# A new order table for a one-core attention and two-layer MLP kernel, drawn with other TensorE durations for the float32 tiles

## The chip, the cores and the metric

The kernel runs on one core of a Trainium2 chip. The metric is the device time of one execution in microseconds (us), given as the median over several runs; lower is better. The profile is of one execution on that core. Its engines are TensorE (PE), VectorE (DVE), ScalarE (ACT), GpSimd (POOL) and SyncE (SP), which only issues DMAs here.

## The reference

```python
q_bucket, k_bucket = sign bits of (q @ proj), (k @ proj), 6 bits each
mask = q_bucket[:, :, :, None] == k_bucket[:, :, None, :]
scores = np.where(mask, q @ k.T / sqrt(64), -1e9)
attn = softmax(scores)
x = (attn @ v)                       # 2 batches, 8 heads, 768 tokens, head size 64
x = x.transpose(0, 2, 1, 3).reshape(1536, 512)
h = maximum(maximum(x @ w1, x @ w2), x @ w3) @ w_out        # 512 -> 768 -> 512
out = elu(h @ w_in) @ w_out2                                 # 512 -> 2048 -> 512
```

Everything is float32 at the interface. The kernel computes products of float32 operands as three float16 products of split halves (high times high, high times low, low times high).

## The kernel before

**Work.** Attention runs over 24 units (`u`: six chunks `c` of 256 tokens, three to a batch, with four pairs of heads `p` each), and each unit has four tiles of 128 queries, so 96 tiles. `plan_tile` (L598 on) writes one tile: four matmuls of scores into one of two score buffers in PSUM (`scores`, L617), the row maximum on DVE (L623), two tiny DVE steps for scale and bias (L624, L626), the exponential on ACT (L628), a float16 high half (L657 on ACT or L659 on DVE), a subtraction for the low half (L663 on POOL or DVE), a DMA transpose issued by SP (L665, tile `PT`), and 18 matmuls with V (L671 to L673). The four tiles of a unit share one output buffer `o` (one buffer in the ring); L689 to L693 scale it, L695 and L696 split it, and an SP transpose (L699) makes the chunk's `xT`.

**The float32 path.** Units 0 to 3 (`u < FU`, FU = 4: tiles 0 to 15) take another way after the exponential: six PE transposes of the float32 tile back into the score buffer (`turn32`, L638/L640), a copy to SBUF (L644), and twelve float32 matmuls with V as loaded (`pv32`, L647/L649).

**V.** `plan_v` loads one pair of heads (L491). In batch 1 all four pairs go through one buffer, `rawv`. A pair's load waits for the split of the pair before (L499, L501); then follow a squared sum on ACT (L332), a one-column matmul that adds it over partitions (`sumsq`, L279/L280), a power-of-two scale (L317, L319) and the split. The first unit of a batch cannot be scaled (L689) before all four pairs of that batch have their scale (L510 to L515).

**The rest.** Each of the six chunks goes through `plan_moe1`: 18 groups of up projections and four of down projections, all by line 712 (12 matmuls of 256 columns for an up group, 18 for a down group), evacuated by L733 to L769; below, U2.0 is the first up-projection group of chunk 2, D1.2 the third down-projection group of chunk 1. Weights are made into float16 halves by L534 to L559. After attention, `plan_moe2` runs 96 groups of 12 matmuls (L712), an ELU chain (L831 to L840) and six matmuls of 512 columns each (L847).

**What sets the order.** Planning gives a list of 3359 operations. `Graph.emit` decompresses `ORDER` into 3359 words; each is an operation's number times eight plus the engine that runs it. Operations are emitted in that order, each to its engine's queue. All queues are in order, and ring buffers are handed out in table order, so the table fixes what stands behind what on each engine. The costs written beside the operations (`PE32T`, `PE32V`, `act`, `gtt` and the others) go into the operation list but `emit` does not read them.

```python
for t, w in enumerate(todo):
    o, e = self.ops[w >> 3], ENGINES[w & 7]
    ...
    o["fn"](e)
```

Of the kernel before, what the change touches and what calls it, by code (L numbers as in the profile page):

```python
# [101 lines left out]

ENGINES = ("PE", "V", "A", "G", "D", "N")
ORDER = (
    "c-l2rOITXx))u_6@y5m*;Ejz}&?w*yh#EknY&6Qo8=DvfOj5BOh&=<b8Hmk5YzE@VKx_w+(}CCy#C9N_4ub7KOb22+5Zi&+48)Uxm=46|f1ZDBdd|!Dt;@UKwKljfU`35Yro!pZ76>PE#r@9H<@K@s"
# [3 lines left out]
    "-85~BIM9u;%Pqe<?lJGapAM`Blejk_+Ud;~$h08vVa7wx^q$!+Q5F~DCG8@0JD;(*0c^$nvp~qNMT2sS=<0`=P;l0MdM-{9{m1TbuC627C|6Zc^GxtBiHLzpj_^MfTsiSj9mX_g1Su7L`#9Rz7C(NC"
    "$IR1<+i{6*_Ol`6`H6~Fv%DG%k#62AmN|TGiJ0%AU28@wE}j<7&PqHsuaC3QMnp01d(NIxKL2@i+b{ZRA2WSWScSIhz|x`Q#^s)QV_#UD^Qf+txi7+)QsYR9I2FIfqw}uCt)2Z3eX7m)8Vy<L^?8=D"  # L110
    "e-i8vGnwrVygE4u4e|VkU;RW**_Kw6X1ZJB#mmEW+b`{Y!uZoM{Wr(f#wN*)L}Qi@vE}b9(>Fdt=!kZRp!!d(r{e91e|7R1@5>9_Eh7*-j@=+M1Qkl&l1?^$I(<S+3%*V+w#_4c)XX@%s6D^f$oxZo"
    "rJyG<nyj;X^Y1=a;V5@AuEInN7s^}ncz=Aofcmb2D<We^9G3HivOTlpoV8(Ce<5>}FRetqYNyNnUix8Qt~XnEAMS8*&nxUrm%(;EzsSXeQm=3$(D!T5D~b9PswDru>HDMT`!A+e4y`Y37n?p!_=IM6"
    "EXLxy*URgE6-}n}{-QqG!3mNR!Tyi=n*IB(udnNIQPdI(oKzh8T)|Kz2|>BK8{PD$jAv)3+x`HXrd<mnB!{f|Qu4Kq<eR4iqPO&8+q~S|H?6vvwn>Dy`zv<ZCV!S0d?l3Fkq_R5Q*_48`{SMLf>1fM"
    "W6ob#8UfecCO-ENwO6Fsi%iS@6K|qp!X1_>`A^2eEXuv&(m&HI!$;b9e!}+3&M#bB7Yf~;>iWky@-}8kn$1}A{k-6h`)E$4%j15ziLr|jbl+<bN^X{eJAJr$W$=~gm*-ZSsc3#|d(HYWY1_0fZhMw|"
    "ep%p9=|2wm7q2+WZ;rnB{RAFU5iA}HtCMshi6nCTQqG7HzeRV+3U-@Fr!)uNifIU2_s#WR+_j%ljLsk_!>3%kYU7#BzVMZ1d8H3?dujsiV2JlMVX<mSllkRJ`Ic|$->2u^mAUDp1-Hlhcx|w5=Rfe*"
    "6#Qe&=Je3^j$i*c#b6$IX1zZ2WNY@bJ>4@dCORX{*1ho0$0v~}Tz2rF+?f0GI({MkS>$jwKF8b62HCUUxvp;ZL(v=Bo7cZ`q<1ml<{=-Rj=9lT{3Nm-P|iCDdY9~oSz}t#MU~cY<k)6^A(8W>-YB}b"
    "j9>jLuE{N?8IaC@nyrT`GSxQw+xeINuVkuE`3pFYaGsPO8?S_caInth-jvAAH*aak_VLHpe{K8&<%R!<EAgfEly`f_Vl_buG#0qfFXnn{hc-TSxlNv?tsREL>GkcobZ1vq8VaB3*}qA%+iLr1ZPpWb"
    "<C!1hc;|c$*;!N?yCh!R-3#y!77cNFfT`K&GF#s)<l5%NUSB92xnB0~|N5r*A{H0P4*#MtRUt91(H)(h|Gs^~UvYdPSK)fnABfIfD1|}KF`c|IOBP<n-m_1OR%pm4@;}y49_~ycDlFt#JdV6W1s3k?"
    "TGCAIl0;C`glOXMZ1pe+czoqe6Xd7QM4MYXjcw+WX^(mZ&e+b?zkfR0vz|n@qp^)%*^dkUpBd48ug~_G|M}JNE#0thKDf!q3x%yV7HxhpqU2&OvGBu%RQ?98C>6f+rT*)qFATAl<~WTsSveSU6ZHut"
    "Q-}V*Wax0^ldE`9^!@KNq5>h{1hLn`Z`WiCDi2P)=3$@9uT<V;=XW)(lRe|vfje|oXZd)p?<P9qcm?nGAAH)y)^{~L*OxztnRBm$@W+xx|J3CwB?dhIwCSaJdVXQsW{bwo<0^bjv9wCGZS21DdZq$&"  # L120
    "<CclBJ`;QqB2TTT4|m#a#2G_Pa?hhNwQTP-d^N4kvx44Gc;Pk@i(gu3JO?Jd76_+oN;<OSBD7kj@L=r&i+!|1nhEYSW_dVc|Jvu@aA>!@r#sHG-GC?<I1Jd~n_hb1j@)<_jj^acCijxGZ)^NPi*<G="
    "36UHf?T5wA)AOh<grE^c>^3Si#srqNR~)}<%SN;M{5~5)>9-<umq3Kt%?7S!CqUn~OFp-n<Uzr)agMM$BtI;ns_%Pe9nQs-r5cILw*JaHubcIqL|6-NiY#$CPhfX4-SANO>}*x8#@+JH@SbJbhI;Za"
    "@Ad^ja(7+pQA~u}W1b&R4nu)`+I}z?J~;pBlBp587ndA+vo84CU-DvcnkjVc+4zFDg19{Kqf^@StbN+yM8xucdL^g1s;!+6OTdlQ9ItuSq?=)dKM>?=4^^CV_*oL#*$V{m0C9R|SDoAj6(NyS{+ly;"
    "q0&Zn13|su`gZY*j3HBm;Wk1`4o4AmcAn-4iDu@VtKuv7qSG~NX>wmEOwPFamM$$4A}B8Kz;{h-V_UAqBz$6Z&&x9^@p9{aaBgu~cIgXo39?454TUA~KL~OX<?a%$dAIrEMkx1KXZ8<6o8h%@lt%O7"
    "vWL!0LS0<xlva<CwPLf)Y`vl*@lSt#eIC7XGud1$d@Qm%&JT~n(Ku~8qG(+3#xO)Zx4as$MgvQV=zHJl`oXdL2KB%_Bl7tDF^xw5+N&bGK89@9XlC222zeT@*?E2}c%+S93+ohWRh%X~J;zzkUDvvW"
    "sM#2cC-DSAi&V0*ZpGK{N~|=U5+%*H4TIhF%ImW@ygv2x-kwCh*69l{Ub*G^z*b-xZkA;ZX|pd1M4AJW&wuj;JTYmAed+gUr+qzsvN7wh_d3om1HtK7d`lPHv7ONomVe9Ta9##H+y3*_OV@S0jjwfk"
    "kAlC5q#k+r`g|o$tD%Q5=>@TN?NQ;1O%)R*ZVfc28$nN|5U#gqM};%?W&_S(=r@jeetXY~qTDmb%)V1k21AOdD{weZz&H3G3fGtXD>c3oAwr86_=eLJ+r6bD>!caw{fo`j?+Q&uUtm8bIaG(jH*z|;"
    "X)t4ROq3fpSp`DtWsMikrAw_{cqz8IX%Y97G8~29rgo;)vkY$4?P0z8#^$@yI=I{ZE&X?-WopTcS!d$5)%7ip_w`{gDMb5p4$dKC2V3`BMaN-acN_f?`(^Ba&BFo_p@bVfKDB9rES^5>i$n!6q3o}t"
# [24 lines left out]


# [818 lines left out]
```

## Time and profile before

| | |
|---|---|
| median of 3 runs | 678.61 us (676.53 to 683.07) |
| the profiled execution | 676.07 us |
| its span, first to last instruction | 673.8 us |
| mean granted TensorE clock | 0.981 of full speed |
| PE, DVE, ACT, POOL busy | 633.0, 547.0, 443.0, 205.0 us |

Busy is the time in which an engine had an instruction in work. A wait is put down to the engine that released it. PEclk is the granted share of TensorE's full clock of 2.4 GHz; 0.50 is its other level, 1.2 GHz. Tile names are the program's, without buffer numbers.

### The profile page before, as it was taken

To read this page: it belongs to the slowest core of one execution; us is meant where nothing else is said; L and a number is where in the kernel's file an instruction comes from. 1 tells how busy PE (TensorE), PEld (TensorE's weight loads), DVE (VectorE), ACT (ScalarE), POOL (GpSimd) and SP (SyncE) were. 2 spreads that over 40 slices of the span, in tenths; PEclk is the share of its full clock that TensorE was granted. 3 is DMA by queue.
4 is the path that set the end of the run, shared out by engine and by line. 5 is a ranking of instruction groups with operands and counts; after the bars stand their busy time and mean duration, and the time that the engine had idled before them with its cause. 6 is when DMAs were issued, how large, how long until landed. Compare 5 with 4: busy or idle time off the path is not lost.

```text
span 673.8 us, 16505 instructions
## 1 busy us (share of the span) xinstructions
PE 633.0 (94%) x6414; PEld 493.8 (73%) x6414; DVE 547.0 (81%) x1538; ACT 443.0 (66%) x825; POOL 205.0 (30%) x184
## 2 busy tenths in 40 slices
...
GB/s 257 270 162 143 130 231 222 176 139 186 134 138 159 153 41 158 167 192 164 156 145 145 225 142 123 96 70 88 64 1 64 94 2 1 1 1 1 33 79 78
DMA packets 176030, 81.35 MB, mean 121 GB/s; under 512 B 142672, under 2 KB 170320, under 8 KB 175952
## 3 DMA queue, kind: packets, MB, share of 16 engines
...
q8 instruction: 50, 0.82, 0.5%
...
## 4 chain that ended last, share of the span: by engine, by line
PE 62%; DVE 3%; DMA 2%; ACT 2%; issue 1%; POOL 0%; DVEq 0%; ACTq 0%; POOLq 0%; SPq 0%
PE mo L712 36%; PE out L847 18%; PE s L620 4%; DMA PT<-hl 1%; PE o L671 1%; PE o L672 1%; PE o L673 1%; DVE m L623 1%; ACT junk L332 1%; DMA rawv<-in_v_dram 0%; ACT P L628 0%; ACT hl L657 0%; DVE dc L545 0%; PE mo L409 0%; DVE hl L663 0%
## 5 line engine op out<-in xcount | busy, mean ns | idle before, releaser
L712 PE MATMUL mo<-xT,w 128*128 128x256 f16 x1296 | 154.9, 275 | 2.8 <-DVE vs L317 2.4
L712 PEld LDWEIGHTS <-w 128*128 128x128 f16 x1296 | 125.3, 99 | 21.5 <-issue 3.8
L663 POOL TENSOR_TENSOR hl<-P,hl 128x768 f16<-128x768 f32 x66 | 109.2, 1663 | 99.6 <-ACT hl L657 58.4
L712 PE MATMUL mo<-x1T,win 128*128 128x256 f16 x1152 | 136.2, 273 | 0.0
L847 PE MATMUL out<-wo2t,gt 128*128 128x512 f16 x576 | 134.7, 379 | 0.0
L712 PEld LDWEIGHTS <-win 128*128 128x128 f16 x1152 | 111.8, 98 | 23.7
L628 ACT ACTIVATE P<-s,bias,scale 128x768 f32<-128x768 f32 x96 | 94.7, 988 | 37.5 <-DVE bias L626 22.3
L840 POOL TENSOR_TENSOR gt<-g,gt 128x256 f16<-128x256 f32 x49 | 34.9, 718 | 231.5 <-DVE gt L838 111.7
L623 DVE TENSOR_REDUCE m<-s 128x1 f32<-128x768 f32 x96 | 91.0, 950 | 12.2 <-PE s L620 11.7
L847 PEld LDWEIGHTS <-gt 128*128 128x128 f16 x576 | 55.2, 98 | 53.6
L831 ACT ACTIVATE r<-mo,nih 128x256 f32<-128x256 f32 x96 | 44.5, 468 | 70.4 <-PE mo L712 66.3
L657 ACT CAST hl<-P 128x768 f16<-128x768 f32 x65 | 53.1, 829 | 16.9 <-DMA PT<-hl 15.0
L834 DVE TENSOR_SCALAR uu<-e,sg 128x256 f32<-128x256 f32 x96 | 36.9, 387 | 26.7 <-ACT e L833 26.4
L671 PE MATMUL o<-vt,PT 128*128 128x65 f16 x480 | 52.8, 196 | 4.4 <-DMA PT<-hl 2.3
L620 PE MATMUL s<-ka,qa 128*128 128x384 f16 x192 | 48.7, 336 | 5.3 <-ACT P L628 3.5
L672 PE MATMUL o<-vt,PT 128*128 128x64 f16 x480 | 52.8, 197 | 0.0
L673 PE MATMUL o<-vt,PT 128*128 128x65 f16 x480 | 52.6, 195 | 0.0
L671 PEld LDWEIGHTS <-PT 128*128 128x128 f16 x480 | 45.5, 99 | 5.9 <-DMA PT<-hl 3.3
L620 PE MATMUL s<-kb,qb 76*128 76x384 f16 x192 | 49.1, 338 | 0.5 <-DMA qb<-btq 0.5
L836 DVE SCALAR_TENSOR_TENSOR g<-mo,aj,uu 128x256 f32<-128x256 f32 x96 | 45.8, 480 | 4.4 <-POOL gt L840 0.5
L672 PEld LDWEIGHTS <-PT 128*128 128x128 f16 x480 | 45.4, 99 | 3.9 <-issue 2.2
L673 PEld LDWEIGHTS <-PT 128*128 128x128 f16 x480 | 45.5, 101 | 0.0
...
## 6 DMA issues: line engine op xcount, KB each, us to landing
...
```

What stands on the lines that cost most here:

```text
L620: PE.matmul(ps.ap[:, h, :NK], lh[0:n, h0 + i, j], rh[0:n, i, h * CH:(h + 1) * CH], start=first, stop=not first)
L623: op({"V": vred(S)}, lambda e: V.tensor_reduce(out=m.ap, in_=ps.ap[:, :, :NK], op=ALU.max, axis=AX.XY), rd=[ps], wr=[m], prio=t + 80.5)
L628: op({"A": act(S, ap=2, acc=int(u < FU)) - 42}, lambda e: A.activation(out=P.ap.rearrange("p (c n) -> p c n", c=2), in_=ps.ap[:, :, :NK], ...
L657: A.copy(hl.ap[:, 0], P.ap)
L663: op({"G": gtt(S), "V": (vtt(S), -109.46)}, lambda e: eng[e].tensor_tensor(out=hl.ap[:, 1], in0=P.ap, in1=hl.ap[:, 0], op=ALU.subtract), r ...
L671: PE.matmul(oo, pt.ap[:, kt], vt.ap[:, i, kt, :D + 1], start=(kt == 0), stop=False)
L672: PE.matmul(oo[:, :D], pt.ap[:, kt], vt.ap[:, i, kt, D + 2:], start=False, stop=False)
L673: PE.matmul(oo, pt.ap[:, NS + kt], vt.ap[:, i, kt, :D + 1], start=False, stop=(kt == NS - 1))
L712: PE.matmul(o, lh(kk, x), rh(kk, y), start=(kk == 0 and pi == 0), stop=(kk == n - 1 and pi == 2))
L831: op({"A": act(NQ, ap=1) - 42}, lambda e, m=m, o=o, r=r: A.activation(out=r.ap, in_=o.ap[:, :NQ], func=AF.Relu, scale=nih.ap[:, m:m + 1]), ...
L836: op({"V": vstt(NQ)}, lambda e, m=m, o=o, uu=uu, gg=gg: V.scalar_tensor_tensor(out=gg.ap, in0=o.ap[:, :NQ], scalar=aj.ap[:, m:m + 1], in1= ...
L847: PE.matmul(outs[j].ap, gt.ap[:, x, j * 128:(j + 1) * 128], wo2t[f].ap[:, y], start=(len(seen) == 1 and pi == 0), stop=(len(seen) == n and ...
```

## The change

The string `ORDER` is replaced as a whole, and one line of constants changes. Nothing else does: the 3359 operations, the buffers and the ring sizes are the same.

```diff
 ENGINES = ("PE", "V", "A", "G", "D", "N")
 ORDER = (
-    "c-l2rOITXx))u_6@y5m*;Ejz}&?w*yh#EknY&6Qo8=DvfOj5BOh&=<b8Hmk5YzE@VKx_w+(}CCy#C9N_4ub7KOb22+5Zi&+48)Uxm=46|f1ZDBdd|!Dt;@UKwKljfU`35Yro!pZ76>PE#r@9H<@K@s"
...
+    "c-lQyOITXx))u_6@y5m*8*gm9vC$at$|h<6O~OWvfLG8cV48~QKx_wMG7y`A*bKyzf!Gejb|AI`@pK@z1F;>5?LbTiVmlB|2I9#;Ob3#a|9Sqk&H4Yezi)l-`>uDb4UgNcWz6SqKV$!(5=mvVN=j#N"
...
 )
...
 TINY = 70
 FU = 4
-PE32T, PE32V = 250, 140
+PE32T, PE32V = 140, 222
 KAPPA = 5.35559
```

Decompressed word by word, the two tables differ as follows. PE runs the same 694 operations in another order.

| operations on | before | after |
|---|---|---|
| DVE | 1533 | 1488 |
| ACT (with its DMA issues) | 753 (30) | 776 (20) |
| POOL | 169 | 181 |
| SP | 208 | 218 |

Moves by kind: the high half of a tile (L657/L659) ACT to DVE 14, DVE to ACT 11; the low half (L663) POOL to DVE 8, DVE to POOL 11; the halves of the ELU (L838) ACT to DVE 20, DVE to ACT 29, and (L840) POOL to DVE 22, DVE to POOL 30; the subtraction of a down projection (L769) POOL to DVE 2, DVE to POOL 5; weight words (L538/L539) ACT to DVE 8, DVE to ACT 20.

Places in the table, 0 to 3358, that the prediction speaks of:

| | before | after |
|---|---|---|
| second V pair of batch 1: load, squared sum, its matmul | 952, 1010, 1037 | 996, 1032, 1094 |
| last V pair of batch 1 to be loaded (p = 2): split before it, load, squared sum, its matmul | 1339, 1340, 1341, 1342 | 1205, 1212, 1243, 1281 |
| first PV matmuls behind it that need `o` (tile 52) | 1351 | 1313 |
| the two subtractions L769 of chunk 0's first down-projection groups, engine | 1030 and 1033, DVE | 974 and 1066, POOL |
| U1.4 | 1043 | 988 |
| first up group of chunk 0 and the PE operation ahead of it that is no small group | 552, tile 22's scores | 539, tile 20's scores |

Between the last load (1212) and its matmul (1281) PE's queue now has D1.2, D1.3, three PV, two scores, U2.0, U2.1, U2.2 and four small groups; between that matmul and tile 52's PV it has two scores, one PV, a small group, U2.3 and U2.4.

## Rows read from the trace of the kernel before

**Rows 1.** The page's first part: busy time, share and instructions of each engine.
```profile
PE 633.0 (94%) x6414; PEld 493.8 (73%) x6414; DVE 547.0 (81%) x1538; ACT 443.0 (66%) x825; POOL 205.0 (30%) x184
```

**Rows 2.** Busy time by stretch; the first line names the columns.
```profile
core 0: us, PE busy (x) PEld busy (x) DVE busy (x) ACT busy (x) POOL busy (x), PEclk, DMA share, GB/s
50.00:88.00 38.00, 33.42 (x304) 28.54 (x302) 36.61 (x97) 35.40 (x62) 8.06 (x7) 1.00 0.53 161
101.00:140.00 39.00, 37.28 (x500) 31.34 (x498) 37.05 (x95) 35.36 (x56) 22.61 (x15) 1.00 0.90 192
157.10:226.90 69.80, 62.75 (x855) 52.61 (x852) 55.87 (x147) 50.63 (x81) 33.24 (x23) 0.95 0.70 149
181.20:188.00 6.80, 4.22 (x20) 2.64 (x21) 5.62 (x13) 2.65 (x3) 6.08 (x4) 0.50 0.54 127
190.00:240.00 50.00, 49.37 (x614) 42.15 (x612) 39.70 (x99) 37.62 (x60) 22.74 (x17) 1.00 0.66 138
246.10:256.30 10.20, 5.48 (x79) 4.72 (x79) 3.62 (x14) 1.87 (x3) 0.00 (x0) 0.50 0.45 86
262.00:378.00 116.00, 114.57 (x1530) 97.88 (x1528) 91.72 (x227) 72.88 (x111) 64.84 (x46) 1.00 0.82 170
378.00:520.00 142.00, 141.88 (x1137) 106.39 (x1136) 121.67 (x379) 99.96 (x226) 20.86 (x26) 1.00 0.28 88
```

**Rows 3.** PE's waits from 174 to 190 us: total us, times, longest.
```profile
PE mo L444 <- DVE bitsk L440: 2.9, 1, 2.9
PE mo L712 <- DVE vs L317: 2.4, 1, 2.4
PE o L671 <- DMA PT<-hl: 1.1, 1, 1.1
```

**Rows 4.** Timeline, 181 to 184 us: start, us, engine, line.
```profile
181.10 0.72 DVE L769 TENSOR_TENSOR x1T<-hx,x1T 128x512 f16<-128x512 f32 x1
181.19 2.12 POOL L663 TENSOR_TENSOR hl<-P,hl 128x768 f16<-128x768 f32 x1 [10.17 <-ACT hl L657]
...
181.86 2.00 DVE L769 TENSOR_TENSOR x1T<-hx,x1T 128x512 f16<-128x512 f32 x1
...
183.91 0.14 DVE L317 TENSOR_SCALAR vs<-mo 128x1 int32<-128x1 int32 x1
```

**Rows 5.** PE's waits from 240 to 262 us.
```profile
PE mo L279 <- ACT junk L332: 5.4, 1, 5.4
PE o L671 <- DVE xf L693: 2.0, 1, 2.0
```

**Rows 6.** Timeline, 243 to 252 us.
```profile
243.69 1.01 DVE L501 SCALAR_TENSOR_TENSOR vt<-rawv,vs,vt 128x768 f16<-128x768 f32 x1
244.72 0.41 SPq L491 DMA_DIRECT2D rawv<-in_v_dram  x1
247.88 0.84 ACT L332 ACTIVATE junk<-rawv 128x768 bf16<-128x768 f32 x1 [4.52 <-DMA rawv<-in_v_dram]
...
248.87 0.16 PE L279 MATMUL mo<-vacc,ones 128*128 128x1 bf16 x1 [5.35 <-ACT junk L332]
...
251.02 0.21 PE L671 MATMUL o<-vt,PT 128*128 128x65 f16 x1 [1.95 <-DVE xf L693]
```

**Rows 7.** The chain that ended last: start, us, what.
```profile
205.51 1.31 PE mo L712 x12
...
214.35 1.97 PE mo L712 x18
...
252.22 4.74 DMA PT<-hl
```

**Rows 8.** Groups by line: busy us, mean ns, then idle before.
```profile
L649 PE MATMUL o<-wot,hl 128*128 128x64 f32 x192 | 23.4, 273 | 0.0
L640 PE MATMUL s<-ident,P 128*128 128x128 f32 x96 | 13.9, 286 | 0.6 <-ACT P L628 0.4
L838 DVE CAST gt<-g 128x256 f16<-128x256 f32 x59 | 16.8, 288 | 2.5 <-DVE g L836 0.5
L838 ACT CAST gt<-g 128x256 f16<-128x256 f32 x37 | 14.6, 400 | 25.4 <-DVE g L836 21.0 <-DVE o2s L319 1.6 <-PE out L847 1.6
```

More of the change, by code (lines that the diff above doesn't have):

```diff
@@ L109 @@
[L109 to L128, printed above, removed]
@@ new lines @@
+    "UYZxbaC_pfyb0VH#K#-Q{hL!L@yD)|EQI>ufz@F1o3Y)KSzPaUb6yn;&OCQ6#%A5uPUiA=F1Li6?m6)kt}A@s`|GDDxx3zQy0__k`*)Pktj44}ISg~}>3gp*<Qw!iGxo@|sC-`@Q!JXP_>nHIxOP*_"
+    "Roys4;5BgO2-XzyrGa()oa>XK<R4~Lxc8|EI}ljad@;UnBlI%6^yj&H^Wo2!Qu8#Vo)4?^$Ajj`nQkc>NxwSwYa@oM^Xr)5<jv$~%S=CJet`#PhOHjtEoUn5s|h=ro!;|W@x8w$dEq%b?pO%!FK+mj"
+    "jf9(3>+yuV&Mn`%EOrszj_*Z&R52#^FqUg;o{R3!U?F@3f8jFCi@%xwT^e?~E`Ih{CB%yjw?`r;HWya+13O+)9Xi;FD%7^{*}KR~Dzc`~z0$Q`gmw)Rp)0fPa^eU3kMZ}D_9eH>G2==2O1Y#N_D(NQ"
+    "{-3qR1fAm-<E+zVUNIRQJF5tSPPn6-#a_?GyKM}!e7MHlfvrioIT+fb7@H?ZU;;hWJ?C4mt+orZpp1;$ncFtw<+JpFSRDMFm<%bcClb6`T6JbmVE&tOIQ7WV(BJ3^3sVZe4L;_e;zK$1Lmh4ttHao-"
@@ new lines @@
+    "?r68UmJ`Jd5!Ibqk(n2qpcb^!_PJO{WD|xB&z72xH_uRW#4X{!u*Rp5W&E4f8O9g07oIP#7ffC+xv8jq=kr^acNEcp?ZA$IKzVx}bx8c%OI$vGqMMu}V&*?wYf|r}L+&<DM?P$L3|k4#^*LqdKUC`Y"
+    "{DrS$g0ZmfUqt+i+(2&}^Bu$z74DgD#;K##F{AER+s2=p>|=v#-C~b8u$?yx*XB~+p`P)I`60@6ZT@PlKKlANwu2oEBH@2du+YeN=Letr&-wlUH;DYAeSWkWGf3WFGxwJni70YLoJ;WqvPvm8Cs;jG"
+    "u9Nyp<;=gltn?Wl6^ifdeu*02vV!7uJ}P)A(XeJqi3u4z0^vneY%W~2oeerJS9F}c=>N=zH>AIj2xYE4vu<PW7XQGVE{q5WKln*m?V!@Fx3x#tf+}KW)lk>zF?oNSQ^n-I!*lP1ukA;FLhM4ecN}+r"
+    "rRr2O77w)J2KFoD^|fuAnH1JU%zr7OcE|1l#nmNr8e*1$;32YfJ@qwOhHbDI<Hu7z;j`!3H}8?nIrO{8DHpzNU?Q*`3|c-HXvLQXGr^YDJr}LTIkM#=Wq^0}x;d!F(2!bcJrPXcx~i>X$(eyvp4jRa"
@@ new lines @@
+    "?c#sQm~Ot=bB<3Kl(UKJ-m~x3Z^hAtS*iB#tr*vK&M-Vnm}Y#4O}*L~CMPdDf8oSmFzhn61Djp=fd5X^uDTX2PM7?Lr*5xlL352TeLd@b>t5TijdieWN71ykxlK>!>%lGmJa)ueuf@6B$G9R;y&Q=6"
+    "ep4*`b?6Tkm=glgnCHM-7Sd|0val^;bg^cLZ^CtRzRk<%?>jNc-uGOk{67?5_f=e$q*XD-5t+^SD)gu2h4x5fus>CE-<;}H)V8s7))ZJ-Fld6WywheZv}S&c=t?KX7mgE7BGu98GIBM(_(eQ68<E<k"
+    "#N?TBaR#L@caLz@BQ`9$PnW$O-bVEAt@G%Vv#xnLcI?@Zc)ZVizMh>IyK!cGkM$dlV*A=@gW2jhy>#L`zZ^xUeiE}yJFaWH)pl)XeEEmsvi8p0@5JswobeLj3jTSF%tzLJ{=hZk5Yc7-u@a7Oc?cd|"
+    "Kt)nQd$8&MN4vT(%9km><(Do}N4jqU$HD4aGW_Q9eUi~ElPRwRM+)lc7lgEp95l}(d@DM$st}&fO5jEQx#b6^+O4muce&&1(;lr!wHc>QHX;ni*0R&!GP{1VT5VGk$GvZ*9xwIl=d4rT4vM{+`4Sh`"
@@ new lines @@
+    "`tMw>Jdf_3GIhq6yl8CI8)vf5V*+9?7?&N*4l?%5R-H}44uvDx@acbBnNeT0&lO67e@r{bRj*R^m5+N!>7y^zMrDC_Oe+Y#I{Vh}u58o4=U@C!;C%5jG<Xz?9}@=(DMjiG39qOAVozUN!VJWGysSp~"
+    "I)hn+|7&((-c{xHJUyMrS#*267avY1?QiSXCsZ3YhqEIA*;?N6Y##g3!Jo{RJD1OAF=6D_XlxMPrYz4d?^g-w??-$4X4`kyOpev-^V=AqnP<D<Nc4OU3)VK{bBZ)sOcGbVsG2_@O@~VAD~5jElf!<+"
+    "^Sw4M>Tqh@A2=YS=+w;EXV|+hk1pd3guC$P@?Ww^_(QmS%r7k?J*TtI9g+Qw%k6dS8!gpqPd6^VupXT{m!{8s(VyMdN(Lg3IHvi#zF<fz6DbDa{+)l<QnO}j?q6rot9bV3%;kFJ=KRvC+^gBvjT-~6"
+    "PFTSi(@W2!6@7i$+#dDDSu4IB>aE*@$!xe@H4|ePh$XLXH#p;X6AHg)a`?5Di&^};sw;&-6B&;)=3V>C!&`?o`xUa~XKTzB4tI4!Hx!=GPtIX>#Cz)C1rGMMaUu{r$G6<#NHi8>bYB0UcLol_Qjgzj"
@@ new lines @@
+    "BSik7GXX(sNuvcjJUNSKjS@6!iOF4lYd{+H*?7yA_txb^59<RvwzlE(Zv}-0R57UDvrh%Z6H+ps#KeR;htp(ToDkZMR_4}}#txB`ocH?XkEdMP9ouvyI%9EgX8FRwE2m|`{>w2T-G@iY<|OSoj<X$)"
+    "*XMqQF8zAp)WuKdT&|T(43D|vd*=s7S8OFUFLvSNwx8NFd}e}&<3ve#!=B*8lx_9s#O^r#F`#xc5W7QiaYfF|@tqr6ucc@HFBStXkH8gYh-(jm9Cr30&R-{AD|bR6O1HJ+6xBuo!R7N4<-v(uNu3TJ"
+    "g?U%ebG_j`1Bo4TBiQ)Vlr^>;2!;c}(`fwtjKfJ>z7H{$m<Xyw+?ERo;zThVpPb<f<}j!0>(#_EDXL=_<SO`m9NUzecJ`z)6@hu;nxM`rTKP5<{@3=naPQ!{nrWbPQh371b4$oN6DGFU<n$aesfhd="
+    "#Z(Kf_1~95?zIGpi7Fy$_V=6buMnM1XyjHIaEBSg?Yjp~$q}Kk=^bI$vggELF;Cc5#FvrT1u41YR;uP-Uc6iKcv)O>T3vU>$7MwH$ZYlL_l?^to?5B*+U)fQ?gS6ra_iKyqm!ub>cqQfJ^N`l5?zVK"
```

53 lines of the change are left out of this document (27 added, 26 removed).

## The prediction

> **What bounds the kernel now.** I read the page's totals first: PE is busy 633.0 of 673.8 us [rows 1], so a new order of the same operations can at most take away PE's idle time and what PE lost at its lower clock. Second, busy time by stretch shows where that is [rows 2]. From 378 us on (378 to 520: 141.88 of 142 us) PE has no gap, so 296 us of the span can only get worse; 262 to 378 (114.57 of 116) and 190 to 240 (49.37 of 50) are nearly as full. Before 140 us PE is not the limit: from 50 to 88 us DVE is busy 36.61 of 38 us and ACT 35.40, PE 33.42; from 101 to 140 DVE 37.05 of 39. What is left are two holes, 174 to 190 and 240 to 262. Third, PE's waits there, and fourth the timeline, to see what each wait hangs on.
>
> First hole: waits of 2.9 + 2.4 + 1.1 = 6.4 us [rows 3]. The 2.4 us ends when DVE gets to L317, 0.14 us of work that frees the PSUM buffer for U1.4; DVE is late because two subtractions of L769 stand ahead of it, the second of which took 2.00 us where the first took 0.72, while POOL ran L663 (2.12 us) [rows 4]. In this hole the clock fell to its 1.2 GHz level: from 181.2 to 188.0 us PEclk is 0.50, and PE was busy 4.22 us of that [rows 2], so 2.1 us were lost by the clock. Sum: 8.5 us.
>
> Second hole: waits of 5.4 + 2.0 = 7.4 us [rows 5]. The timeline is plain: the split L501 ends at 244.70, the load of the next V pair is issued at 244.72, its squared sum starts at 247.88, its matmul at 248.87, and the PV matmul that needs `o` at 251.02 [rows 6]. These operations stand directly behind one another in the old table (places 1339 to 1342, 1351), so nothing on PE covers the load. Here PEclk is 0.50 from 246.1 to 256.3 with 5.48 us busy [rows 2]: 2.7 us lost. Sum: 10.1 us.
>
> **The change part by part.** No operation is added or removed; what counts is what stands ahead of what.
>
> The second hole. The new table splits the last-but-one pair at 1205, issues the load at 1212, squares at 1243 and adds at 1281. The price to hide is 4.15 us, from the issue at 244.72 to the matmul at 248.87 [rows 6]. Between load and matmul PE's queue has two down groups of 1.97 us and three up groups of 1.31 [rows 7]: 7.9 us, and three PV and two scores beside. That covers it with over 3 us to spare even if the load landed as late as the slow transposes do (4.74 us [rows 7] instead of some 3.1). From the matmul to the next `o`, 2.15 us are needed (248.87 to 251.02), and PE has two up groups, 2.6 us, with two scores and a PV. If this cover fails for want of DVE (it is the same queue L501 stands in), all 10.1 us return. I take -10.1 us; ends -10.1 and 0. SP now issues this load at 1212; behind it SP holds the chunk's `xT` transpose (1228). SP waits there for the split at 1205, which is 7 places older: I cost it at nothing, covered by the 7.9 us; if the split is late, the transpose is late by the same and U2.0 with it.
>
> The first hole. Both L769 go to POOL, earlier and later (974, 1066), U1.4 moves ahead (988), and the V pair's load, squared sum and matmul lie at 996, 1032, 1094 with many PE groups between. Between the matmuls of the key bits and their transpose (the 2.9 us wait) there are now an up group and a PV, some 1.9 us, where there was a PV. So the 2.4 and the 2.1 of the clock go, of the 2.9 I leave 1.0, and the 1.1 (a transpose that lands late) I leave too. Sum -8.5 + 2.1 = -6.4; ends -8.5 and 0.
>
> The float32 stage and chunk 0. The new costs do not reach the chip but shape the table: the trace has 23.4 / 16 = 1.46 us busy for the twelve matmuls of a `pv32` and 13.9 / 16 = 0.87 for the six transposes [rows 8], against 0.84 and 1.50 us in the old constants, 1.33 and 0.84 in the new. But the stage is DVE's and ACT's [rows 2], and what the table puts ahead there counts. Adding for every operation its own duration less its overlap (for one that moves, the mean of its kind on the other engine), DVE has 81.5 us of work ahead of tile 20's scores in the old table and 81.6 in the new, ACT 77.7 and 79.1: nothing gained. Ahead of the last up group of chunk 0, at 140 us, DVE has 127.3 and now 124.5, ACT 122.7 and 120.5. So some 2.5 us less work of the two bound engines, with the same PE work done. Against it: PE, in order, now reaches chunk 0's first up group directly behind tile 20's scores, and waits for its `xT`. Behind it stand tile 22's and 23's scores, for which DVE and ACT wait. The chain to it from the last `pv32` is three short steps (L693, L695, L696) and a transpose, with some 3.5 us of PE work beside it (two scores, a `gram` and small groups, at 0.65 us for a tile's scores); the short steps take about half of that, so with a transpose of 4.74 us [rows 7] it would be some 3 us late, part of it under DVE work that is due anyway. I take -2 us; ends -5 and +3.
>
> From 262 us. The halves of the ELU are spread anew, net 9 of L838 to ACT (0.400 us instead of 0.288 [rows 8]) and 8 of L840 to POOL. All DVE work falls by some 19 us, ACT's rises by 15, POOL's by 12. While PE is full and ACT busy 99.96 of 142 us [rows 2], this is hidden; it costs if a chain into the next product gets longer than the groups beside it, at most one group of 1.31 us each time. I take +0.5 us; ends 0 and +4.
>
> Waits that the new order makes elsewhere: before, 190 to 240 us had 0.63 us of PE idle and 262 to 378 had 1.43 [rows 2], so a drawing costs about that much where it goes well. I saw no pair of operations in the new table as tight as load, square and matmul were. +1 us; ends 0 and +9 (one hole like the first).
>
> Sum: -10.1 - 6.4 - 2 + 0.5 + 1 = -17.0 us, on the profiled execution's 676.07: 659.1. That execution lies 2.54 us under the median of the runs shown, 678.61; taken off the median, the forecast is 661.6 us.
>
> **A rule weighed.** POOL gets twelve more subtractions. In the row, a two-input subtraction on DVE took 2.00 us beside POOL's, not 0.72, so 1.28 more [rows 4]. The Trainium skill ("SBUF — State Buffer", section "Who interferes with whom") says that a DVE instruction with two SBUF inputs and a GpSimd one that reads SBUF exclude each other, the later one standing still to the end. That row agrees with it, in that DVE's ended 0.55 us after POOL's. By that rule the sum would be the third rival's.
>
> **The rivals.**
> (1) A new hole. Queues shift, and one chain, most likely scores to transposed tile in the stretch 157 to 227 us, opens a wait like the first hole with its fall of the clock: +8.5. For it: a tile there passes five engines and two DMA queues in order, and one late operation holds all behind it; in both holes the clock fell after waits of a few us. Against: the chains have more PE work between them than before. Time: 661.6 + 8.5 = 670.1.
> (2) All given back, by the engines that bound the float32 stage: ACT and DVE lose there what I count as gained (+3 for -2, so +5), chunk 0's first up groups stall once more with a fall of the clock (+8.5), and the late chains cost 4 for 0.5: 661.6 + 17 = 678.6, no change. For it: ACT gets 15 us more work, and it was at 35.40 of 38 us. Against: only some 1.4 us of that stand ahead of tile 20.
> (3) Slower, by POOL and DVE shutting each other out. Place: between tile 40's scores and U2.0, where POOL's work rises from 30.2 to 38.4 us by the table and DVE's falls from 58.8 to 46.2. If none of it overlapped, the stretch would need 38.4 + 46.2 = 84.6 us; by the forecast it takes 69.8 - 8.5 + 2.1 = 63.4. That is +21.2, and the second hole's gain is then lost as well, since its chain runs over DVE: 661.6 + 21.2 + 10.1 = 692.9. It ends slower than before once 17 of these 31.3 us are paid. Against: in the old stretch DVE 55.87 + POOL 33.24 = 89.1 us fit into 69.8 [rows 2], so at least 19.3 us did overlap. As some overlap will stay, I put the rival at 688.
>
> **How the numbers follow.** The forecast's own ends: all at their best, 661.6 - 2.1 - 3 - 0.5 - 1 = 655.0, less some 5 us for the spread of single runs (676.53 to 683.07 before), 650; at the other side 667, with a few of the small terms at their worse end. Its chance is 0.63. Rival 1, 667 to 672: 0.17. Rival 2, 672 to 685: 0.13. Rival 3: 0.07. A measurement of this kernel tells about 1%, 6.8 us, from no change. Faster by more than that (under 671.8): 0.63 + 0.17 = 0.80. Same: 0.13. Slower: 0.07. The range leaves out rival 3, the upper half of rival 2 and a little at the bottom, 0.18 in all: 649 to 676. The cases of the other sign hold little, so the likeliest one's own range is 650 to 667 within it.
>
> **What would show it.** Right: no wait of PE on L332 behind a `rawv` load over 1 us; no wait on L317 or L440 over 2 us between 160 and 190 us; PEclk 1.00 in both stretches; the span from the first ELU group to the end unchanged, about 270 us, so that the gain stands before 378 us; DVE still over 0.93 busy from 50 to 130 us. Wrong: a PEclk of 0.50 somewhere after 100 us, a wait of PE over 2 us there, or idle PE time after 378 us. A time under 650 would mean that the float32 stage got shorter, which I hold to be bound by DVE.

## The result, and the profile after

The new table takes 646.15 us (median of 4 runs, 644.94 to 649.86) against 677.78 for the kernel before beside it (4 runs, 676.53 to 683.07): a ratio of 0.9528, 95% interval 0.9464 to 0.9593. Faster, as forecast, but by nearly twice as much as forecast (661.6), and below the range (649 to 676). The profiled execution took 646.06 us, its span is 644.3; before, 676.07 and 673.8. So 30.0 us have to be found. (After, and in some of the runs, line numbers are higher by one, since the string takes a line more: L333 there is L332 before.)

The page's totals and its row of PE slices, after; they answer to [rows 1]:

```profile
PE 624.7 (97%) x6414; PEld 490.8 (76%) x6414; DVE 528.0 (82%) x1493; ACT 454.8 (71%) x858; POOL 218.5 (34%) x196
...
PE   4999889999999999999999999999999999999997
```

PE's busy time fell by 8.3 us though it runs the same 6414 matmuls. Some 6.3 of that is work no longer done at 1.2 GHz: before, PE was busy 15.9 us in its three stretches at half clock, which cost half of that; after, 3.3 us in one. The other 2.0 are not traced. The rest of the gain, 21.7 us, is idle time. DVE lost 19 us of work, ACT gained 12 and POOL 13.5, much as the counts of the tables said.

Busy time by stretch shows where. To compare like with like I cut both runs at the same PE operations: the last up group of chunk 0 (140.3 us before, 131.9 after), the first of chunk 1 (160.1 and 152.9), U2.0 (226.9 and 209.2), tile 70's scores (282.2 and 250.2), the first ELU group (403.9 and 374.1). The work between two cuts is nearly the same, not quite, as the orders differ (748 and 795 matmuls in one row). After:

```profile
core 0: us, PE busy (x) PEld busy (x) DVE busy (x) ACT busy (x) POOL busy (x), PEclk, DMA share, GB/s
50.00:88.00 38.00, 33.56 (x301) 28.57 (x300) 36.58 (x102) 37.16 (x65) 9.38 (x9) 0.98 0.67 183
88.00:132.00 44.00, 43.76 (x563) 37.09 (x563) 42.84 (x115) 43.69 (x70) 29.75 (x20) 0.97 1.00 202
152.90:209.20 56.30, 55.78 (x748) 47.70 (x746) 47.34 (x121) 47.91 (x79) 36.40 (x27) 1.00 0.96 181
209.20:250.20 41.00, 41.00 (x553) 34.96 (x552) 36.34 (x95) 29.96 (x47) 24.97 (x18) 1.00 0.77 153
250.20:374.10 123.90, 123.83 (x1539) 107.75 (x1536) 97.11 (x249) 83.09 (x141) 53.60 (x37) 1.00 0.72 166
```

The same cuts in the kernel before:

```profile
88.00:140.30 52.30, 47.77 (x584) 38.59 (x583) 49.93 (x131) 48.30 (x75) 29.77 (x20) 0.93 0.91 195
160.10:226.90 66.80, 59.75 (x795) 50.14 (x791) 53.22 (x138) 48.18 (x77) 30.24 (x22) 0.95 0.72 154
226.90:282.20 55.30, 46.85 (x570) 39.43 (x567) 37.44 (x94) 31.27 (x46) 26.52 (x19) 0.91 0.65 128
282.20:403.90 121.70, 120.67 (x1502) 104.31 (x1499) 96.24 (x250) 79.35 (x131) 52.19 (x38) 1.00 0.72 166
```

Read each row as span less PE busy. Both holes are gone: idle 0.52 and 0.00 us after, 7.05 and 8.45 before. And a third place that I had not counted as a hole has gone with them: from 88 us to the end of chunk 0 PE is busy 43.76 of 44 us, where it was busy 47.77 of 52.3, part of that at half clock. From 50 to 88 us nothing changed in kind (33.42 of 38 before [rows 2]).

PE's waits over the whole run, after: total, times, longest.

```profile
PE mo L297 <- DMA rawq<-in_q_dram: 3.7, 1, 3.7
PE s L621 <- ACT P L629: 1.9, 2, 1.6
PE s L641 <- ACT P L629: 1.7, 4, 0.8
```

The first is the start of the kernel. Nothing here answers to [rows 3] or [rows 5]; between 152 and 190 us PE waits for nothing at all. The V chain of the second hole [rows 6] now reads, in the timeline after:

```profile
201.68 0.54 SPq L492 DMA_DIRECT2D rawv<-in_v_dram  x1
206.56 0.84 ACT L333 ACTIVATE junk<-rawv 128x768 bf16<-128x768 f32 x1
213.09 0.17 PE L280 MATMUL mo<-vacc,ones 128*128 128x1 bf16 x1
```

From issue to matmul 11.41 us pass where 4.15 passed before, and none of it shows on PE: the matmul has no idle time before it. What was late before is early now by being started earlier.

**One measure for all runs.** To place a gain or a loss in a table with another order, I use the time that PE has lost by the start of a given group: its start less the full-clock durations (means from the trace of before) of all PE work that the table places ahead of it. Other durations shift a whole column alike, so what counts is how two rows differ. Worked out so for the profiled execution of each kernel, in us:

| | tile 20 | last up group, chunk 0 | first, chunk 1 | U2.0 | tile 70 | output group 90 |
|---|---|---|---|---|---|---|
| before | 31.6 | 38.2 | 39.2 | 49.2 | 61.1 | 63.1 |
| after | 29.3 | 30.4 | 31.0 | 32.1 | 32.4 | 33.5 |
| new engines, old places | 48.6 | 67.6 | 74.4 | 87.5 | 104.2 | 132.3 |
| new places, old engines | 42.5 | 51.8 | 58.2 | 66.3 | 72.2 | 102.1 |
| new to 924, then old | 32.1 | 33.8 | 34.4 | 46.9 | 58.3 | 61.7 |
| old to 909, then new | 34.4 | 46.7 | 48.5 | 49.4 | 49.8 | 51.8 |
| old, V chain early | 31.7 | 38.3 | 39.4 | 50.0 | 56.1 | 57.8 |
| old, L769 on POOL | 32.0 | 38.5 | 39.4 | 48.7 | 60.7 | 62.4 |
| new to 536, then old | 32.1 | 44.6 | 46.1 | 56.9 | 68.9 | 70.5 |
| old to 549, then new | 31.9 | 37.7 | 38.3 | 38.9 | 39.2 | 40.9 |
| new, four up groups late | 28.2 | 34.3 | 34.9 | 35.3 | 35.7 | 37.3 |
| new, V chain late | 27.5 | 30.4 | 30.9 | 32.4 | 39.2 | 40.7 |
| old, both mends | 31.3 | 37.8 | 39.0 | 48.2 | 54.0 | 55.5 |
| new, old ELU engines | 27.3 | 29.3 | 29.8 | 30.9 | 31.3 | 39.4 |

The first two lines give the gain by stretch: 2.3 to tile 20, 5.5 from there to the end of chunk 0, 0.4 to chunk 1, 8.9 in the stretch of the first hole, 11.6 in that of the second, 0.9 behind: 29.6 of the 30.0 us.

### The profile page after: what moved, and what is told of

It is laid out like the page before. It is cut to its first block, busy times and chain, and to the rows that moved or that the text cites. A ratio compares the mean times of both kernels' runs of the same rounds, so it can differ in the third digit from the quotient of the medians.

```text
span 644.3 us, 16489 instructions
## 1 busy us (share of the span) xinstructions
PE 624.7 (97%) x6414; PEld 490.8 (76%) x6414; DVE 528.0 (82%) x1493; ACT 454.8 (71%) x858; POOL 218.5 (34%) x196
## 4 chain that ended last, share of the span: by engine, by line
PE 80%; DVE 4%; ACT 4%; DMA 3%; issue 1%; POOL 0%; DVEq 0%; SPq 0%; ACTq 0%
PE mo L713 47%; PE out L848 19%; PE s L621 6%; PE o L672 2%; PE o L673 2%; PE o L674 2%; ACT P L629 1%; DVE m L624 1%; DMA kb<-ka 1%; DMA rawv<-in_v_dram 1%; PE mo L410 1%; DMA PT<-hl 1%; ACT hl L645 1%; DVE hx L734 0%; ACT mo L535 0%
## 5 line engine op out<-in xcount | busy, mean ns | idle before, releaser
L713 PE MATMUL mo<-xT,w 128*128 128x256 f16 x1296 | 152.6, 272 | 0.0
L664 POOL TENSOR_TENSOR hl<-P,hl 128x768 f16<-128x768 f32 x69 | 115.0, 1674 | 64.9 <-ACT hl L658 31.5
L713 PEld LDWEIGHTS <-w 128*128 128x128 f16 x1296 | 123.6, 98 | 16.7
L841 POOL TENSOR_TENSOR gt<-g,gt 128x256 f16<-128x256 f32 x57 | 39.3, 695 | 213.2 <-ACT gt L839 125.4
L624 DVE TENSOR_REDUCE m<-s 128x1 f32<-128x768 f32 x96 | 91.1, 951 | 12.6 <-PE s L621 11.2
L835 DVE TENSOR_SCALAR uu<-e,sg 128x256 f32<-128x256 f32 x96 | 35.5, 371 | 26.3 <-ACT e L834 25.7
L658 ACT CAST hl<-P 128x768 f16<-128x768 f32 x62 | 50.7, 830 | 2.9 <-DMA PT<-hl 2.4
L672 PE MATMUL o<-vt,PT 128*128 128x65 f16 x480 | 51.3, 193 | 0.2
L673 PE MATMUL o<-vt,PT 128*128 128x64 f16 x480 | 51.3, 194 | 0.0
L674 PE MATMUL o<-vt,PT 128*128 128x65 f16 x480 | 51.1, 192 | 0.0
L837 DVE SCALAR_TENSOR_TENSOR g<-mo,aj,uu 128x256 f32<-128x256 f32 x96 | 46.1, 482 | 6.0 <-POOL gt L841 2.0
L621 PE MATMUL s<-kb,qb 76*128 76x384 f16 x192 | 48.2, 332 | 1.0 <-DMA kb<-ka 1.0
L672 PEld LDWEIGHTS <-PT 128*128 128x128 f16 x480 | 44.4, 96 | 2.7 <-DMA PT<-hl 0.4
L673 PEld LDWEIGHTS <-PT 128*128 128x128 f16 x480 | 44.3, 97 | 2.1
L713 PEld LDWEIGHTS <-wot 128*128 128x128 f16 x432 | 41.4, 98 | 5.6
```

Of the source, the lines that this page charges most:

```text
L621: PE.matmul(ps.ap[:, h, :NK], lh[0:n, h0 + i, j], rh[0:n, i, h * CH:(h + 1) * CH], start=first, stop=not first)
L624: op({"V": vred(S)}, lambda e: V.tensor_reduce(out=m.ap, in_=ps.ap[:, :, :NK], op=ALU.max, axis=AX.XY), rd=[ps], wr=[m], prio=t + 80.5)
L658: A.copy(hl.ap[:, 0], P.ap)
L664: op({"G": gtt(S), "V": (vtt(S), -109.46)}, lambda e: eng[e].tensor_tensor(out=hl.ap[:, 1], in0=P.ap, in1=hl.ap[:, 0], op=ALU.subtract), r ...
L672: PE.matmul(oo, pt.ap[:, kt], vt.ap[:, i, kt, :D + 1], start=(kt == 0), stop=False)
L673: PE.matmul(oo[:, :D], pt.ap[:, kt], vt.ap[:, i, kt, D + 2:], start=False, stop=False)
```

## The experiments

Two theories stood at first. The places alone: what stands ahead of what makes the gain, and the engines that changed hands are incidental. The engines alone: DVE was relieved, and the order is incidental. Each was given half of the change.

**New engines, old places.**

```diff
 every entry at its place in the old table
-V L838 ... (and 360 other operations, each on its old engine)
+A L838 ... (on its engine in the new table)
```

> The old table's places with the new table's engines: each operation stands where it stood before, but runs on the engine the new table names. Theory A (places make the gain): the second hole stays whole, since load, squared sum and matmul of the last V pair still stand side by side (10 us lost there); the first loses the wait behind the two L769, which now run on POOL, at most 4.5 us with the clock; the stage before 140 us gains at most 2. About 672 us, ratio 0.985 to 1.00. Theory B (the 19 us less DVE work make the gain): the float32 stage, bound by DVE, gets shorter and the waits on DVE go: 655 us or less, ratio 0.97 or less.

Measured: 737.41 us, ratio 1.0842 (1.0772 to 1.0912). **New places, old engines**, the mirror image:

```diff
 every operation on its engine in the old table
-its place in the old table
+its place in the new table
```

> The new table's places with the old table's engines. Theory A: nearly the whole gain stays, 646 to 654 us, ratio 0.955 to 0.965; PE's wait on L333/L332 behind a rawv load is under 1 us and no stretch after 100 us is at 1.2 GHz. Theory B: most of the gain goes, 665 us or more, ratio 0.98 or more, with DVE busy 547 us as before.

Measured: 712.3 us, ratio 1.0442 (1.0386 to 1.0498). PE's waits in the first:

```profile
PE s L620 <- ACT P L628: 22.5, 21, 3.5
PE mo L279 <- ACT junk L332: 7.4, 4, 5.5
```

and in the second:

```profile
PE s L621 <- ACT P L629: 11.1, 12, 2.1
...
PE out L848 <- DVE gt L841: 3.2, 3, 2.3
```

Either half of the change alone makes the kernel slower by 8 and by 4%. Tile after tile the scores wait for the exponential of an earlier one. Both theories fall, the one of the engines by the first run and the one of the places by the second: a place is drawn for the engine that an operation has, since on an engine in order it stands behind that engine's other work, and one half of a table is no table.

**Cutting the table in two.** The first 924 entries new, then the old order and engines for what is left:

```diff
-c[0:924] of the old table
+c[0:924] of the new table
 all entries not among these, in the old order
```

> The first 924 entries of the new table (up to tile 40's scores, with all of chunk 0's up and down groups), then everything else in the old table's order. If the stages add up, as the two traces have it: the time to the first up group of chunk 1 falls by some 8 us (160.1 to 152 us) and both holes come back, 668 to 671 us, ratio 0.985 to 0.99. If the head only shifts work that is paid later, the time is 676 or more; if it is the cause of the rest, under 660.

Measured: 673.11 us, ratio 0.9877 (0.9839 to 0.9914). And the first 909 old, the rest new:

```diff
 c[0:909] of the old table
-all entries not among these, in the old order
+all entries not among these, in the new order
```

> The first 909 entries of the old table, then everything else in the new table's order: the counterpart of the run before. If the stages add up: both holes gone (some 21 us), the head as before (tile 40's scores at about 157 us), 654 to 658 us, ratio 0.965 to 0.97. If the head is what keeps the holes shut: 665 or more, with a wait of PE over 2 us after 160 us.

Measured: 659.51 us, ratio 0.9687 (0.9633 to 0.9741). In the first both holes are back, by PE's waits:

```profile
PE mo L280 <- ACT junk L333: 5.2, 1, 5.2
...
PE mo L445 <- DVE bitsk L441: 3.6, 1, 3.6
PE mo L713 <- DVE vs L318: 2.4, 1, 2.4
```

In the second, from 160 to 262 us, this is all:

```profile
PE s L620 <- ACT P L628: 0.5, 1, 0.5
PE mo L430 <- DVE hx L765: 0.5, 1, 0.5
```

So the stretches earn for themselves, if each has both halves of its own table: 8.4 us in the head and 21.3 behind it by the ratios (of 680.21, the kernel before beside these runs), together 29.7, near the 32.0 that the change gives by its own.

**The second hole, from both sides.** In the old table I moved only the chain early, with the six small DVE operations behind it that end in the scaling of `o`:

```diff
-1339 V L501   1340 D L491   1341 A L330   1342 PE L276   1343 V L317 ...
+1247 V L501   1247 D L491   1277 A L330   1307 PE L276   1307 V L317 ...
```

> The old table with one chain moved: the split of the last-but-one V pair (L499, L501), the load of the next (L491), its squared sum (L330), its matmul (L276) and its release (L317, L319), which stood at 1339 to 1344, go to 1247 to 1308, and the six DVE operations of the unit behind them to 1308; nothing else moves and no engine changes. If the second hole was this chain standing side by side, the wait of 5.4 us on L332 and the half clock of 246.1 to 256.3 us go and the time falls by 8 to 10 us, to about 669. If the hole only shows that the whole stretch is late on DVE or ACT, the wait moves to the next scores or PV and the time falls by less than 3 us.

Measured: 673.03 us, ratio 0.9884 (0.9819 to 0.9949), 7.9 us by the ratio. PE's waits from 235 to 265 us:

```profile
PE s L620 <- ACT P L628: 2.6, 2, 1.4
PE o L671 <- DMA PT<-hl: 1.3, 1, 1.3
```

The 5.4 us wait is gone, and so is the half clock of 246.1 to 256.3 us. But smaller waits come up behind it: from U2.0 to tile 70 PE now loses 6.1 us, where it lost 11.9. The mirror image in the new table, the chain and what stands behind it put side by side again:

```diff
-1205 V L501   1212 D L491   1243 A L330   1281 PE L276   1284 V L317 ...
+1304 V L501   1304 D L491   1304 A L330   1304 PE L276   1304 V L317 ...
```

> The new table with the last V pair's chain side by side again: the split L501 (1205), the load (1212), squared sum (1243), matmul (1281) and its release, and the six DVE operations behind it, all at 1304, ahead of tile 52's PV at 1313. If the distance in the table is what closed the second hole, the wait on L332 is back with some 4 to 5.4 us, the clock falls, and 7 to 10 us are lost (about 655). If the new order closes it because PE's queue stands further behind the other engines, the load lands under PE's backlog and under 3 us are lost.

Measured: 653.52 us, ratio 0.9646 (0.9617 to 0.9676). Its timeline shows [rows 6] again:

```profile
217.38 0.54 SPq L492 DMA_DIRECT2D rawv<-in_v_dram  x1
220.63 0.84 ACT L333 ACTIVATE junk<-rawv 128x768 bf16<-128x768 f32 x1 [3.95 <-DMA rawv<-in_v_dram]
...
221.62 0.16 PE L280 MATMUL mo<-vacc,ones 128*128 128x1 bf16 x1 [4.80 <-ACT junk L333]
```

The two agree: between U2.0 and tile 70 this one chain's place is worth 5.8 us of lost time in the old table and 6.5 in the new. The rival, that in the new table the load would land under PE's backlog, falls.

**The first hole.** Only the two L769 to POOL, in their old places:

```diff
-1030 V L769   1033 V L769
+1030 G L769   1033 G L769
```

> The old table in its old order, with only the two subtractions of L769 at places 1030 and 1033 on POOL in place of DVE. If the 2.4 us wait on L317 was their price, it goes, and with less waiting the clock may hold: 2 to 4.5 us faster, with the 2.9 us wait on the key bits left. If POOL and DVE hold each other up, or POOL is late with the L663 that stand behind, no gain or up to 3 us slower.

Measured: 675.9 us (10 runs), ratio 0.9957 (0.9916 to 0.9999). PE's waits from 165 to 195 us:

```profile
PE mo L444 <- DVE scale L624: 2.2, 1, 2.2
PE o L671 <- DMA PT<-hl: 1.8, 1, 1.8
```

The wait on L317 has gone, another on L624 has come, and the clock still fell (0.50 from 178.3 to 188.5 us). The interval goes from no gain to 6 us and so does not choose between the two expectations; by lost time, 9.3 us from chunk 1 to U2.0 against 10.0, little is gained. Then both holes' mends together, with U1.4 ahead of the transposed key bits:

```diff
 the V chain early, as above
-1030 V L769   1033 V L769   1043 PE U1.4
+1024 G L769   1027 G L769   1034 PE U1.4
```

> The old table with three edits: the V chain moved early as in the run of that alone; the two L769 at 1030 and 1033 on POOL, at 1024 and 1027; U1.4 from 1043 to 1034, ahead of the matmul of the key bits' transpose. If the two holes are worth what the forecast gave them and can be mended by themselves, 8 from the V chain and 5 to 8 from the first hole: 662 to 666. If a mended wait in the first hole only passes to the next operation, as with L769 alone, the time stays at 668 to 672.

Measured: 670.02 us, ratio 0.9894 (0.9851 to 0.9937): no more than the V chain alone. From 165 to 200 us:

```profile
PE mo L279 <- ACT hl L657: 2.0, 1, 2.0
PE mo L444 <- DVE vs L317: 1.0, 1, 1.0
```

Each wait passes to the next operation, and PEclk is 0.50 from 182.4 to 189.2 us again. The stretch loses 9.2 us up to U2.0, where it lost 10.0. So the first hole is no matter of the two L769 and one group. Old to 909 and then new shows that the entries behind 909 close it (0.9 us lost there); which of them is open.

**The float32 stage and chunk 0.** The first 536 entries new (to tile 20's scores):

```diff
-c[0:536] of the old table
+c[0:536] of the new table
 all entries not among these, in the old order
```

> The first 536 entries of the new table (the float32 stage, to tile 20's scores), all others in the old order with the old engines. If the gain lies in the stretches where PE's lag fell, this is worth 2 to 3 us (about 676), the lag at the first up group of chunk 1 is about 37, and both later holes are there. If the fall of the clock at 92.5 us is a consequence of the order ahead of it, it goes too, and the gain is 5 to 6 us with a lag of about 33.

Measured: 682.69 us (10 runs), ratio 1.0029 (0.9986 to 1.0073). And the old stage with the new order from 549 on:

```diff
 c[0:549] of the old table
-all entries not among these, in the old order
+all entries not among these, in the new order
```

> The first 549 entries of the old table, all others in the new order with the new engines. If each stretch earns for itself, this loses 2 to 3 us against the full change (about 650) with no wait over 2 us behind tile 20. If the later order needs the float32 stage that it was drawn with, waits come back behind tile 20 and the time is over 655.

Measured: 653.14 us, ratio 0.9591 (0.9520 to 0.9661). Neither came out by either of its numbers, so the stage and chunk 0 do not add up as the head and the rest did. The first gains nothing to tile 20 and then loses 12.5 us up to the end of chunk 0 (6.6 before), on waits from 88 to 150 us, behind entry 536, where the two tables meet:

```profile
PE mo L444 <- DVE bitsq L440: 4.4, 2, 2.3
PE s L620 <- DMA qb<-btq: 2.8, 1, 2.8
```

The second loses 7.4 us against the full change by the profiled executions, all of it before chunk 1, and 5.8 of PE's lost time lie between tile 20 and the end of chunk 0, nearly the 6.6 of the kernel before. Its waits from 88 to 140 us:

```profile
PE s L621 <- ACT P L629: 2.0, 2, 1.7
PE mo L713 <- DVE dc2w L546: 1.9, 1, 1.9
```

The second row is the third up group, which waits for its PSUM buffer `mo`. The preparation of another weight held it until then:

```profile
98.93 0.64 ACT L535 ACTIVATE mo<-raww 128x512 f32<-128x512 f32 x1 [1.07 <-DMA raww<-in_moe_w_dram]
100.75 0.68 DVE L546 SCALAR_TENSOR_TENSOR dc2w<-mo,dc2w 128x512 int32<-128x512 int32 x1
```

In the new table these two operations stand inside the float32 stage (477 and 528; in this run 554 and 559), so the group does not meet them. This pointed at the groups themselves, and the next run moves only them:

```diff
-536 S20  539 U0.0  549 U0.1  554 S22  560 U0.2  569 P16  575 U0.3  582 S23
+536 S20  554 S22  569 P16  569 U0.0  569 U0.1  582 S23  582 U0.2  582 U0.3
```

(S is a tile's scores, P its PV, U an up group; the first evacuation goes from 562 to 583.)

> The new table with chunk 0's first four up groups (places 539 to 575) later: two behind tile 22's scores and tile 16's PV (569), two behind tile 23's scores (582), as the old table has them; the first evacuation (562) goes behind them to 583. If these groups fill PE's time between the score tiles, and that is where the stretch from tile 20 to the end of chunk 0 gained, 2 to 6 us are lost by the last up group of chunk 0, with a longer stretch at half clock near 90 us. If the stretch is bound by DVE and ACT as forecast, nothing is lost: within 1 us of the full change.

Measured: 650.64 us, ratio 0.9607 (0.9576 to 0.9638). Its stretch at half clock, and PE's waits from 84 to 140 us:

```profile
86.40:96.60 10.20, 7.92 (x56) 4.99 (x53) 9.54 (x27) 9.94 (x15) 7.27 (x4) 0.50 0.81 184
```

```profile
PE s L621 <- ACT P L629: 3.4, 2, 1.8
PE o L672 <- DMA PT<-hl: 0.7, 1, 0.7
```

From tile 20 to the end of chunk 0 PE loses 6.1 us, against 1.1 after and 6.6 before: four groups set back by at most 30 places give back 5.0 of the 5.5 us that this stretch gained. Three more executions begin as the new table does and lose 1.7 (new to 924), 2.9 (V chain late) and 2.0 us (old ELU engines) here, so the loss stands out from their spread; by the ratios it is some 5 us too, with intervals that just overlap. PE now waits 1.8 us at tile 22's scores, where two of the groups stood. The half clock lasts 10.2 us, with 7.92 busy, so it costs 4.0; after, it lasted 3.4 (86.8 to 90.2). It begins ahead of tile 20's scores in both. DVE has done 120.76 us of work by the last up group of chunk 0 in both runs, 3.9 us later in this one.

**Engines where PE is full.** The new table with the old engines of L838, L840 and L857:

```diff
 every entry at its new place
-L838, L840, L857 on the engines of the new table
+L838, L840, L857 on the engines of the old table (108 differ)
```

> The new table with the old engines of the second MLP's split and add operations alone (L838, L840, L857; 108 operations), all places and all other engines new. If PE is full from 374 us on and hides what engine the ELU halves take, as the forecast has it, the time is within 2 us of the full change. If an operation's place is drawn for its engine there too, 10 to 17 us are lost behind the first output group, as in the run with all the old engines, with waits on gt.

Measured: 652.64 us, ratio 0.9642 (0.9601 to 0.9683). PE's waits from 374 us on:

```profile
PE out L848 <- DVE gt L841: 2.9, 2, 1.9
PE out L848 <- ACT gt L839: 0.9, 1, 0.9
```

From tile 70 on 8.1 us are lost, against 1.1 after; nearly all of that lies behind the first ELU group. The two rows are 3.8 us of it. That is between the two numbers that were expected, and it shows that even in a stage in which PE is full in both kernels, an operation on another engine than its place was drawn for opens waits.

## Why the prediction was right, and where it was wrong

By its terms, from the table above:

| term | forecast | measured |
|---|---|---|
| second hole (U2.0 to tile 70) | -10.1 | -11.6 |
| first hole (chunk 1's first group to U2.0) | -6.4 | -8.9 |
| float32 stage and chunk 0 | -2 | -8.2 |
| from 262 us, and new waits | +1.5 | -0.9 |
| sum | -17.0 | -29.6 |

**Right: the second hole.** It was the chain of split, load, squared sum and matmul, and its distance in the table is what counts; two runs from opposite sides price it at 5.8 and 6.5 us. That the forecast of 10.1 came so near to 11.6 is then in part luck: it put the two largest rows [rows 5] and the whole half clock down to the chain, and some 5 us of the stretch are not the chain's. With the chain early in the old table, 3.9 us of waits on P and PT are there instead; no run shows what in the new order closes those.

**Right in sign, for a poor reason: the first hole.** All of it went, where I left 2.1 us. But the mechanism that I named (L769 ahead of L317, U1.4 behind) does not carry it: mended alone, it gives 0 to 6 us by the interval of L769 alone (0.7 by lost time), and nothing more in the run with U1.4. The V pair's three operations, which the forecast named beside them, were in no run moved alone. The rows [rows 3] showed who was last, not how many stood just behind. What closes this hole stays open, beyond that it stands behind entry 909.

**Wrong: the step "the stage is DVE's and ACT's, and what the table puts ahead there counts".** Of the 12.6 us that the sum missed, 6.2 are here. For the stretch to tile 20 nothing speaks against it: 2.3 us by the profiled executions, and the six executions with the new entries there lost 27.3 to 32.1 us (mean 29.4), the six with the old ones 31.3 to 34.4 (mean 32.2). For chunk 0 it fails. I read a busy share of 37.05 of 39 us on DVE [rows 2] as a bound and priced the stretch by the change of DVE's work ahead alone (-2.8). From tile 20's scores to the last up group, columns as above, these are the kernel before, the new table, the new table with the four groups late, and old to 549, then new:

```profile
93.10:140.30 47.20, 45.48 (x562) 37.12 (x562) 44.94 (x116) 43.23 (x68) 26.02 (x18) 0.93 0.91 196
90.70:131.90 41.20, 41.08 (x544) 35.08 (x544) 40.40 (x108) 40.92 (x65) 27.06 (x19) 1.00 1.00 202
89.60:135.80 46.20, 43.66 (x547) 36.20 (x545) 40.74 (x109) 41.35 (x65) 27.45 (x19) 0.92 0.90 178
93.30:139.20 45.90, 43.07 (x543) 35.97 (x543) 41.71 (x109) 43.39 (x69) 26.54 (x19) 0.96 0.83 189
```

The last two have 3 to 4 us less DVE work than before, nearly as little as the new table, and gain only 1.0 and 1.3 us where it gains 6.0. So less DVE work does not shorten the stretch by itself: 5.0 us hang on where four up groups stand. It is needed all the same, since 44.94 us of DVE work would not go into 41.2 us. After, PE, DVE and ACT are all full there.

What PE lost nearby was, before, a wait of 0.8 and one of 1.7 us, both ahead of tile 20's scores, and then 6.8 us at half clock; after, a wait of 1.6 us ahead of tile 21's scores and 3.4 us at half clock:

```profile
92.50:99.30 6.80, 6.21 (x41) 4.08 (x41) 6.73 (x18) 6.47 (x12) 4.01 (x3) 0.50 0.86 213
86.80:90.20 3.40, 3.31 (x27) 2.30 (x25) 3.26 (x8) 3.37 (x5) 2.68 (x3) 0.50 1.16 205
```

So the clock cost 3.1 us before and 1.7 after. Behind tile 20's scores the new table puts the four up groups between the score tiles, and PE waits for nothing there. I saw that the groups had moved up, and booked it as a risk (the transpose of `xT` late), not as a filling; the first of them starts without a wait for its `xT`. The run with the groups late is the test of it: the same DVE work, 5 us lost.

The term was mis-sized for a second reason. DVE's work ahead of the last up group of chunk 0 was forecast as 127.3 and 124.5 us; the traces have 127.54 and, after, 120.76. So it fell by some 4 us more than the durations of before gave. In part the same small instructions overlap more: the 34 L624 there add 4.71 us to their neighbours, 6.06 before. The rest is spread over other lines.

The forecast's last sign fails with this step: the time is under 650, but the float32 stage itself, to tile 20, gave only 2.3 us of it.

**Right: from 262 us**, and with it what the forecast named as its signs: the whole gain stands by U5.0 (at 378 us before: 62.8 us lost against 32.9), DVE is over 0.93 busy from 50 to 132 us, and no wait of PE behind 100 us is over 0.5. The ELU halves cost nothing, and the groups show the trade that the forecast used; they answer to [rows 8]:

```profile
L839 DVE CAST gt<-g 128x256 f16<-128x256 f32 x50 | 14.4, 290 | 2.9 <-PE out L848 1.3
L839 ACT CAST gt<-g 128x256 f16<-128x256 f32 x46 | 18.2, 399 | 23.8 <-DVE g L837 17.9 <-DVE aj L816 2.0 <-PE out L848 1.6
```

The reason was too simple, though. Not every choice of engine is hidden there: with the old engines in the new places 6 to 7 us came back.

**The rivals.** No new hole opened (first rival), and nothing was given back (second). For the third, POOL and DVE shutting each other out: from chunk 1 to U2.0 PE is idle 0.52 us, so nothing of the 21.2 was paid. DVE's 47.34 and POOL's 36.40 us, 83.7 together, fit into 56.3, so both were busy at once for at least 27.4; by the same cuts before it was 16.7. The L769 that took 2.00 us [rows 4] counted as busy for all of it, so these rows do not say how long the two held each other. The rule that the forecast weighed (the Trainium skill, "SBUF — State Buffer", section "Who interferes with whom") speaks of one pair of instructions; what it takes from a whole stretch, no run here shows.

**The range** failed because all four terms came out at or beyond their best ends together. That they depend on one another is not shown: the head and the rest, run apart, gave 29.7 of the 32.0 us. In both holes the new order took away nearly all idle time and all half clock of the stretch, the small waits that the rows left out among them; the 3.2 us beyond the best end of chunk 0's term are the step above.
